# Block-sparse attention with a mixture of experts: the transposing product of the row maxima one step later, its rows masked by GpSimd

## The chip, the cores and the metric

The kernel runs on one core of a Trainium2 chip. The metric is the device time of one execution in microseconds (us); the time before is the median of three runs. The engines are called PE (TensorE, matrix products; PEld is its weight load), DVE (VectorE), ACT (ScalarE), POOL (GpSimd) and SP (SyncE, which issues most transfers). Each engine works through its own instructions in the order in which the program lists them, and waits on semaphores for the others.

## The reference

Attention over four batches, eight heads, 768 rows and 64 columns a head, then a mixture of eight experts of which each row takes two:

```python
scores = scale * np.matmul(q, k.transpose(0, 1, 3, 2))
mask = np.abs(blk_i - blk_j) <= 1          # blocks of 32, and first and last rows and columns of blocks
for qb in range(n_blocks):
    for kb in sampled_blocks[qb]:          # three sampled blocks a row of blocks
        mask[qb * block:(qb + 1) * block, kb * block:(kb + 1) * block] = True
scores = np.where(mask, scores, -1000000000.0)
scores = scores - np.max(scores, axis=-1, keepdims=True)
attn = np.exp(scores)
attn = attn / (np.sum(attn, axis=-1, keepdims=True) + 1e-09)
x = np.matmul(attn, v)                     # then rows of 512, over the heads
...
noisy_logits = x @ w_gate + noise * np.log1p(np.exp(x @ w_noise))
out[rows of e] += weight * (np.maximum(x @ w1[e], 0.0) @ w2[e])   # the two best experts of each row
```

## The kernel before

The class Attention computes the scores transposed, keys on partitions and query rows along the free dimension, so that exp(scores) can go straight into the product with v as the stationary operand. The maximum of each query row must therefore be known before, and it enters through the score product itself: q2 and k2 have extra contraction rows. Rows 64 to 87 carry the block mask, row 88 a constant, and rows MR = 96 to 101 carry the maxima: row 96 + t of q2 holds the maxima of the query tile t (128 rows) in the columns of that tile and zero in the others, against a constant -64 in k2.

There are 192 steps, six for each of 32 heads; two heads are a group, and 12 steps a group's turn. What a step n does stands in the loop of `steps` (lines 417 to 472), and this listing is the order in which every engine gets its instructions:

- `exp(n, 0)` and `exp(n, 1)` (lines 268 to 280): the scores of one tile of 128 keys against three tiles of query rows each, two products (L277, L279; the second reads k2 and q2 with the maxima) into a PSUM buffer pe (three of them), and ACT's exponential of it (L280).
- `max_mm(m)` (lines 228 to 238): two products (L234, L235) for the maxima of a later query tile m, into a PSUM buffer pm (two of them), and a relu of one half by ACT (L237). `max_red(m)` (lines 240 to 247): DVE adds the halves and takes the maximum along the row (L244) into one column of mn, a tile of 128x128 float16 per head (three of them).
- `halve(n)` (line 285): DVE turns the exponentials into float16.
- `av(n - 3)` (line 311): the product with v, 18 times three parts. Where n - 3 is the last step of a head (n % 6 = 2), this product comes first in the step and not behind `exp(n, 1)`; it then follows that of the step before without a score product between them.
- `av_end`: the end of a head: PSUM copied by ACT, sum and reciprocal (L326, L328) and scaling (L331) by DVE, a high part by ACT and a low part by GpSimd (L340).
- For later groups: casts (ACT, L206, and GpSimd, L208, one step later), transposes and copies by transfers from SP, the split of v (ACT, and DVE at L185) and differences of k (DVE, L254).

The maxima run ahead of the scores by LM = T + 3 = 9 steps (lines 68, 414 and 429; T = 6 query tiles a head): step n makes those of tile n + 9. When the sixth tile of a head has been reduced, `max_red` puts the head on the list `full` (line 247), with mn and the pm buffer of that last tile. In the next step (n % 6 = 3, three steps ahead of the head's first scores), behind the next tile's `max_mm`, `row_mm` (lines 256 to 260) transposes mn by a product with the identity into the free columns 384 to 511 of that same pm buffer (L260), and at the end of the step, behind `max_red` and `halve`, `row_put` (lines 262 to 266) has DVE read the six rows from PSUM, six times over, multiply them with a diagonal of the identity, and write the 6x768 values into q2 (L265). `start` (lines 396 to 402) does the same in the prologue, for the first eight tiles.

Between these parts `background(n, spot)` is called at four spots of a step. At spots 0 to 2 it advances a generator, Router.run, which computes the routing of one batch and ends with twelve indirect transfers by GpSimd (L695, each behind a small memset, L694) that scatter slots into a table in memory. The generator is advanced once a spot, and twice from step 158 to step 173 (lines 1060 to 1063); between two scatters it yields five times, for the third batch twice. At spot 3 the plan of `at(...)` is carried out: at step 169 a memset by GpSimd (L735), at step 178 the load of the first experts' table rows (L786), from step 180 on the indices made of them (DVE, L799) and the gathers of rows (GpSimd, L815).

Behind the attention the experts run one after the other (class Experts); this part holds over half of the span and is not changed.

Of the kernel before, what the change touches and what calls it, by code (L numbers as in the profile page):

```python
# [9 lines left out]
F32 = mybir.dt.float32  # L10
F16 = mybir.dt.float16
# [5 lines left out]
ALU = mybir.AluOpType  # L17
AX = mybir.AxisListType
PSUM = bass.MemoryType.PSUM
P = 128  # L20
# [24 lines left out]
class Attention:  # L45
# [16 lines left out]
    def __init__(self, tc, q, k, v, sampled):  # L62
        self.tc, self.nc = tc, tc.nc
        self.q, self.k, self.v, self.sampled = q, k, v, sampled
        self.B, self.H, self.S, self.D = q.shape
        self.T = self.S // P
        self.NB = self.S // 32
        self.LM = self.T + 3
        self.NG = self.B * self.H // self.G
        self.NSTEP = self.B * self.H * self.T  # L70
        self.st = {}
        self.todo = {}
        self.full = []
        self.now = 0

    def open(self, ctx, early):
# [151 lines left out]
    def max_mm(self, n):  # L228
        g, h, t = self.where(n)
        r = self.st[g]  # L230
        K = 64 + self.NB
        pm = self.ps_m.tile([P, 2, 512], F32, name="pm")
        q = r["q2"]
        self.nc.tensor.matmul(pm[:, 0, 0:384], q[0:K, h, t, :], r["k2"][0:K, h, 0::2, :], start=True, stop=True)  # L234
        self.nc.tensor.matmul(pm[:, 1, 0:384], q[0:K, h, t, :], r["kd"][0:K, h], start=True, stop=True)  # L235
        rl = self.sm.tile([P, 384], F32, name="rl")
        self.nc.scalar.activation(rl, pm[:, 1, 0:384], AF.Relu)  # L237
        self.st["pm", n] = pm, rl

    def max_red(self, n):  # L240
        g, h, t = self.where(n)
        pm, rl = self.st.pop(("pm", n))
        mn = self.mn[(n // self.T) % 3]
        self.nc.vector.tensor_tensor_reduce(rl, pm[:, 0, 0:384], rl, 1.0 / 64.0, -3.0e38, ALU.add, ALU.max,  # L244
                                            accum_out=mn[:, self.MR + t:self.MR + t + 1])
        if t == self.T - 1:
            self.full.append((g, h, mn, pm))

    def diff(self, g, hs):
        D = self.D  # L250
# [2 lines left out]
        k = r["k1" if g else "k2"][0:D, hs].rearrange("p g (j w) c -> p g j w c", w=2)  # L253
        self.nc.vector.tensor_tensor(kd[0:D, hs], k[:, :, :, 1], k[:, :, :, 0], op=ALU.subtract)  # L254

    def row_mm(self):
        self.rows, self.full = self.full, []
        n = self.MR + self.T
        for g, h, mn, pm in self.rows:
            self.nc.tensor.matmul(pm[0:n, 0, 384:512], mn[:, 0:n], self.ident, start=True, stop=True)  # L260

    def row_put(self):
        T, s = self.T, slice(self.MR, self.MR + self.T)
        for g, h, mn, pm in self.rows:
            self.nc.vector.tensor_tensor(self.st[g]["q2"][s, h], pm[s, 0, None, 384:512].to_broadcast([T, T, P]),  # L265
                                         self.ident[s, s, None].to_broadcast([T, T, P]), op=ALU.mult)

    def exp(self, n, x):
        nc, T = self.nc, self.T
        g, h, c = self.where(n)  # L270
        r = self.st[g]
        if x == 0:
            self.st["p32", n] = self.pi.tile([P, T, P], I32, name="p32")
        p32 = self.st["p32", n]
        t = slice(3 * x, 3 * x + 3)
        pe = self.psum()
        nc.tensor.matmul(pe[:, 0:384], r["k1"][:, h, c, :], r["q1"][:, h, t, :], start=True, stop=False)  # L277
        K = self.MR + T
        nc.tensor.matmul(pe[:, 0:384], r["k2"][0:K, h, c, :], r["q2"][0:K, h, t, :], start=False, stop=True)  # L279
        nc.scalar.activation(p32[:, t].rearrange("p t c -> p (t c)"), pe[:, 0:384], AF.Exp, scale=0.125)  # L280
# [12 lines left out]
    def later(self, steps, f):  # L293
        if steps:
            self.todo.setdefault(self.now + steps, []).append(f)
        else:
            f()
# [46 lines left out]
    def start(self, mi):  # L344
        nc, D, NB = self.nc, self.D, self.NB
        s32 = self.sampled.bitcast(I32)
        sb = mi.tile([P, NB * 3, 2], I32, name="sb")
        nc.scalar.dma_start(sb.rearrange("p a b -> p (a b)"),
                            bass.AP(tensor=s32.tensor, offset=s32.offset, ap=[[0, P], [1, NB * 6]]))
        nc.scalar.preload_act_table_set("natural_log_exp_and_others")  # L350
        r = self.st[0] = {nm: self.raw.tile([P, self.G, self.T, D], F32, name="raw_" + nm) for nm in "kq"}
        for h in range(self.G):
            for nm, src in (("q", self.q), ("k", self.k)):
                nc.sync.dma_start(r[nm][:, h], src[0, h].rearrange("(p t) d -> p t d", p=P))
        self.load(1, nc.sync, "kq")
        self.masks(mi, sb)
        self.constants(True)
        kn, qn = self.nat[0]
        kb, qb = self.kb, self.qb
        r["k2"], r["q2"] = self.k2[0], self.q2[0]  # L360
        self.new(r, "k1")
        self.new(r, "q1")
        cast = lambda dst, src: nc.scalar.activation(dst, src, AF.Copy)

        def high(h):
            cast(qb[:, h, :, 0:D], r["q"][:, h])
            cast(kb[:, h, :, 0:D], r["k"][:, h])

        def both(h):
            nc.gpsimd.tensor_sub(kn[:, h, :, D:], r["k"][:, h], kb[:, h, :, 0:D])  # L370
            nc.gpsimd.tensor_sub(qn[:, h, :, 0:D], r["q"][:, h], qb[:, h, :, 0:D])
            cast(kn[:, h, :, 0:D], r["k"][:, h])
            cast(qn[:, h, :, D:], r["q"][:, h])

        high(0)
        self.turn(r["q2"], qb, 0, "AA")
        both(0)
        high(1)
        both(1)
        self.load(0, None, "v")  # L380
        self.split(1, 0)
        self.split(1, 1)
        self.constants(False)
        self.split(1, 2)
        self.split(1, 3)
        self.turn(r["k2"], kb, 0, "AD")
        self.diff(0, slice(0, 1))
        more = {0: [(self.turn, r["k1"], kn, 0, "AD"), (self.load, 1, None, "v")],
                1: [(self.turn, r["q1"], qn, 0, "AD"), (self.load, 2)],
                2: [(self.turn, r["q2"], qb, 1, "AD")],  # L390
                3: [(self.turn, r["k2"], kb, 1, "AD")],
                4: [(self.diff, 0, slice(1, 2)), (self.load, 3)],
                5: [(self.vsplit, 0, 0)],
                6: [(self.turn, r["k1"], kn, 1, "AD"), (self.vsplit, 0, 1)],
                7: [(self.turn, r["q1"], qn, 1, "AD")]}
        for n in range(self.T + self.XM):
            self.max_mm(n)
            self.row_mm()
            self.max_red(n)
            self.row_put()  # L400
            for f, *a in more.get(n, ()):
                f(*a)
        self.flush()
        for t, m in ((self.k2, self.MR + self.T), (self.q2, self.MR)):
            nc.sync.dma_start(t[1][D:m], t[0][D:m])
        self.split(1, 4)
        self.split(1, 5)
        self.nmax = self.T + self.XM
        self.plan = {0: [(self.vsplit, 0, 2)], 2: [(self.diff, 1, slice(0, self.G))], 3: [(self.load, 2, None, "v")],
                     4: [(self.vsplit, 1, 0)], 5: [(self.vsplit, 1, 1)], 6: [(self.vsplit, 1, 2)],  # L410
                     9: [(self.vsplit, 2, 0)], 10: [(self.vsplit, 2, 1), (self.load, 3, None, "v")], 11: [(self.vsplit, 2, 2)],
                     1: [(nc.sync.dma_start, t[2][D:m], t[0][D:m]) for t, m in ((self.k2, self.MR + self.T), (self.q2, self.MR))]}
# [4 lines left out]
    def steps(self, on_group, background):  # L417
        NSTEP, LM, LA, GT = self.NSTEP, self.LM, self.LA, self.G * self.T
        for n in range(NSTEP + LA + 6 + self.ROWLATE):
            g, i = divmod(n, GT)  # L420
# [15 lines left out]
                self.exp(n, 0)  # L436
            self.av_end(j, "copy", on_group)
            self.av_end(j - 3, "high", on_group)
            for m in new:
                self.max_mm(m)  # L440
            self.row_mm()
# [3 lines left out]
                self.av(j)  # L445
            background(n, 0)
            self.av_end(j - 1, "sum", on_group)
            for m in new:
                self.max_red(m)
            if n < NSTEP:  # L450
                self.halve(n)
            self.row_put()
            background(n, 1)
            self.av_end(j - 1, "inverse", on_group)
            background(n, 2)
# [734 lines left out]
```

## Time and profile before

| | |
|---|---|
| median of 3 runs | 985.88 us |
| lowest and highest | 981.26 and 986.39 us |
| the profiled execution | 973.13 us, span 971.3 us |
| mean granted TensorE clock | 0.973 |
| PE busy | 876.8 us (90%) |
| DVE busy | 524.2 us (54%) |
| ACT busy | 454.6 us (47%) |
| POOL busy | 346.2 us (36%) |
| row matmul, L260 on PE | 32 times, 259 ns each, 32.6 us of idle time ahead of it |
| masked write into q2, L265 on DVE | 32 times, 962 ns each |
| halving, L285 on DVE | 192 times, 642 ns each |

The shares are means over the whole span, in which the attention and the experts have different limits; the text below goes by stretches. In a row of the waits stands who waited, for which line, and then the sum in us, the times and the longest one. In a row of the groups and of the timeline the operation is followed by output <- inputs, by shape, and in brackets by the idle time ahead of it and what ended that. In a row of a stretch stand the busy us of PE, PEld, DVE, ACT and POOL (with the number of instructions), then the granted clock, the share of the DMA engines and GB/s. Durations of matmuls are modelled: they overlap, and the distance between two starts is the time that each takes.

### The profile page before, as it was taken

What the parts mean: (1) busy time and instruction counts of PE and PEld (TensorE: products, weight loads), DVE (VectorE), ACT (ScalarE), POOL (GpSimd) and SP (SyncE); (2) the same over time, 40 slices, a digit from 0 to 9 for tenths busy, and PEclk for the clock granted to TensorE, in tenths of its full rate; (3) what the DMA queues carried; (4) which work ended last, traced back from release to release, by engine and by line L of the source; (5) the groups of instructions that cost most, each with busy time, mean ns of one, the idle gap of its engine ahead of it and who ended that gap; (6) DMA issues with size and microseconds to landing.
All of it is one profiled execution on the core that took longest, in us unless ns stands there. A gap on an engine that the chain in (4) does not pass through costs nothing. (4 is left out here: it accounts for less than half of the span.)

```text
span 971.3 us, 21082 instructions
## 1 busy us (share of the span) xinstructions
PE 876.8 (90%) x8493; PEld 530.2 (55%) x8493; DVE 524.2 (54%) x1238; ACT 454.6 (47%) x973; POOL 346.2 (36%) x392
## 2 busy tenths in 40 slices
PE   4888998989889887997799999999999999999993
PEld 2566665666566665645455555554554554555541
DVE  6888889989999974744023334333334333333210
ACT  6988888898889784522023123122221231231200
POOL 5432232552264163254242242342432432432220
PEclk9999999999999998997899999999999999999997
DMA  7678776796699288675859378297394593782210
GB/s 204 134 173 190 180 170 154 152 176 165 153 165 175 62 116 149 216 109 140 154 126 240 97 201 180 79 235 171 92 253 120 128 230 108 162 215 97 57 39 31
DMA packets 206618, 145.63 MB, mean 150 GB/s; under 512 B 142197, under 2 KB 183413, under 8 KB 206512
## 3 DMA queue, kind: packets, MB, share of 16 engines
q1 hardware_dynamic: 172848, 78.49, 40.0%
q0 software_dynamic: 14256, 39.58, 13.9%
q10 hardware_dynamic: 19408, 26.13, 11.1%
q8 instruction: 68, 1.11, 0.5%
q14 instruction: 38, 0.31, 0.1%
HBM read 79.62 MB, written 26.32 MB: 109 GB/s over the span
## 5 line engine op out<-in xcount | busy, mean ns | idle before, releaser
L280 ACT ACTIVATE p<-pe 128x384 int32<-128x384 f32 x384 | 189.7, 516 | 43.6 <-PE pe L279 36.9
L869 ACT ACTIVATE hh<-ph 128x408 f16<-128x408 f32 (+2 forms) x136 | 66.8, 492 | 273.7 <-PE ph L864 227.0
L870 DVE SCALAR_TENSOR_TENSOR hl<-ph,hh 128x408 f16<-128x408 f32 (+2 forms) x136 | 76.2, 561 | 180.1 <-ACT hh L869 180.1
L914 POOL DMA_INDIRECT out_dram<-y,mt x56 | 72.9, 1301 | 227.0 <-DVE y L912 105.1
L311 PEld LDWEIGHTS <-p 128*128 128x128 f16 x3456 | 128.5, 99 | 23.1 <-issue 1.7
L884 PEld LDWEIGHTS <-hh 128*128 128x128 f16 x768 | 75.0, 98 | 99.7 <-issue 14.4
L277 PE MATMUL pe<-q,k 128*128 128x384 f16 x384 | 128.2, 334 | 1.4 <-DVE r_A L649 1.0
L279 PE MATMUL pe<-q,k 102*128 102x384 f16 x384 | 128.2, 334 | 0.0
L285 DVE TENSOR_SCALAR p<-p 128x1536 f16<-128x1536 uint16 x192 | 123.3, 642 | 7.3 <-ACT p L280 5.8
L912 DVE SCALAR_TENSOR_TENSOR y<-py,mt,pv 128x512 f32<-128x512 f32 (+2 forms) x56 | 41.2, 748 | 157.9 <-PE py L884 142.2
L244 DVE CUSTOM_DVE_ANT_0 rl<-pm,rl 128x384 f32<-128x384 f32 x192 | 105.9, 552 | 34.3 <-ACT rl L237 30.7
L311 PE MATMUL po<-vx,p 128*128 128x65 f16 x1152 | 123.3, 196 | 0.4 <-DVE p L285 0.4
L311 PE MATMUL po<-vb,p 128*128 128x65 f16 x1152 | 123.0, 195 | 0.0
L311 PE MATMUL po<-vl,p 128*128 128x64 f16 x1152 | 122.8, 194 | 0.0
L864 PE MATMUL ph<-xta,w1hb 128*128 128x408 f16 x512 | 111.0, 340 | 7.3 <-issue 4.3
L237 ACT ACTIVATE rl<-pm 128x384 f32<-128x384 f32 x192 | 99.4, 518 | 11.2 <-PE pm L235 9.5
L830 POOL DMA_INDIRECT pv<-out_dram,gi x56 | 56.7, 1012 | 99.5 <-ACT hh L869 78.6
L864 PE MATMUL ph<-xtb,w1ha 128*128 128x408 f16 (+1 forms) x448 | 91.3, 325 | 0.3 <-DMA xtb<-xg 0.3
L884 PE MATMUL py<-w2ha,hh 128*128 128x512 f16 x192 | 73.9, 385 | 8.5 <-DVE y L912 8.5
L234 PE MATMUL pm<-k,q 88*128 88x384 f16 x192 | 64.7, 337 | 14.3 <-DVE mn L244 10.3
L340 POOL TENSOR_TENSOR x<-xr,x 128x384 f16<-128x384 f32 x32 | 34.5, 1078 | 119.0 <-ACT x L338 108.5
L864 PEld LDWEIGHTS <-w1hb 128*128 128x128 f16 x512 | 50.5, 99 | 47.0 <-issue 6.2
(192 smaller groups left out, 1616.5 us busy)
## 6 DMA issues: line engine op xcount, KB each, us to landing
wraw<-in_moe_w_dram SPq DMA_DIRECT2D x60, 512.0 KB, 4.2
raw_v<-in_v_dram ACTq DMA_DIRECT2D x16, 384.0 KB, 4.2
out_dram<-zero ACTq DMA_DIRECT2D x24, 256.0 KB, 3.6
x_rows<-x SPq DMA_DIRECT2D x16, 384.0 KB, 5.8
raw_k<-in_k_dram ACTq DMA_DIRECT2D x14, 384.0 KB, 3.8
raw_q<-in_q_dram ACTq DMA_DIRECT2D x14, 384.0 KB, 6.8
k<-k SPq DMA_DIRECT2D x15, 192.0 KB, 3.7
q<-q SPq DMA_DIRECT2D x15, 192.0 KB, 3.8
```

What stands on the lines that cost most here:

```text
L237: self.nc.scalar.activation(rl, pm[:, 1, 0:384], AF.Relu)
L244: self.nc.vector.tensor_tensor_reduce(rl, pm[:, 0, 0:384], rl, 1.0 / 64.0, -3.0e38, ALU.add, ALU.max, accum_out=mn[:, self.MR + t:self.MR ...
L277: nc.tensor.matmul(pe[:, 0:384], r["k1"][:, h, c, :], r["q1"][:, h, t, :], start=True, stop=False)
L279: nc.tensor.matmul(pe[:, 0:384], r["k2"][0:K, h, c, :], r["q2"][0:K, h, t, :], start=False, stop=True)
L280: nc.scalar.activation(p32[:, t].rearrange("p t c -> p (t c)"), pe[:, 0:384], AF.Exp, scale=0.125)
L285: self.nc.vector.tensor_scalar(p.rearrange("p t c w -> p (t c w)"), p32.bitcast(U16).rearrange("p t c -> p (t c)"), HC, None, op0=ALU.mult)
L311: self.nc.tensor.matmul(o, p[:, t, :, w], v, start=first and i == 0, stop=last and i == 2, skip_group_check=True)
L864: nc.tensor.matmul(ph[:, b, 0:m], w[wt][:, kb, fs], r["xt"][:, kb, a, o:o + m], start=i == 0, stop=i == last)
L869: self.pace = nc.scalar.activation(hv, ph[:, b, 0:m], AF.Relu)
L870: nc.vector.scalar_tensor_tensor(self.hl[:, f, o:o + m], ph[:, b, 0:m], 0.0, hv, op0=ALU.max, op1=ALU.subtract)
L884: nc.tensor.matmul(py, h[:, f, o], w[x][:, f, :], start=i == 0, stop=i == last)
L914: nc.gpsimd.indirect_dma_start(out=self.out, out_offset=bass.IndirectOffsetOnAxis(ap=r["mt"][0:m, c, 0:1], axis=0), in_=y[0:m], in_offset= ...
```

## The change

The transposing product is made one step later than before, as the first thing in a pm buffer that the step's own maxima need anyway; a head's entry now ages by one step on the list before it is due. So that it is still done three steps ahead of the head's scores, the maxima run one step further ahead (LM = T + 4). In the loop, DVE copies the six rows out of PSUM into a small float16 tile, ahead of the step's maximum (`row_copy`, behind the first background spot), and GpSimd multiplies them with the diagonal and writes q2. The prologue keeps DVE's `row_put`, one pass later.

```diff
-        self.LM = self.T + 3
+        self.LM = self.T + 4
...
-        self.full = []
+        self.full, self.due, self.rows = [], [], []
...
         pm = self.ps_m.tile([P, 2, 512], F32, name="pm")
+        self.row_mm(pm)
         q = r["q2"]
...
         if t == self.T - 1:
-            self.full.append((g, h, mn, pm))
+            self.full.append((1, g, h, mn))
...
-    def row_mm(self):
-        self.rows, self.full = self.full, []
+    def age(self):
+        self.due += [e[1:] for e in self.full if not e[0]]
+        self.full = [(0, *e[1:]) for e in self.full if e[0]]
+
+    def row_mm(self, pm=None):
         n = self.MR + self.T
-        for g, h, mn, pm in self.rows:
+        for g, h, mn in self.due:
+            pm = pm or self.ps_m.tile([P, 2, 512], F32, name="pm")
             self.nc.tensor.matmul(pm[0:n, 0, 384:512], mn[:, 0:n], self.ident, start=True, stop=True)
+            self.rows.append((g, h, pm))
+        self.due = []
 
     def row_put(self):
         T, s = self.T, slice(self.MR, self.MR + self.T)
-        for g, h, mn, pm in self.rows:
+        for g, h, pm in self.rows:
             self.nc.vector.tensor_tensor(self.st[g]["q2"][s, h], pm[s, 0, None, 384:512].to_broadcast([T, T, P]),
                                          self.ident[s, s, None].to_broadcast([T, T, P]), op=ALU.mult)
+        self.rows = []
+
+    def row_copy(self):
+        T, s = self.T, slice(self.MR, self.MR + self.T)
+        for g, h, pm in self.rows:
+            tm = self.sm.tile([P, P], F16, name="tm", bufs=2)
+            self.nc.vector.tensor_copy(tm[s], pm[s, 0, 384:512])
+            self.nc.gpsimd.tensor_tensor(self.st[g]["q2"][s, h], tm[s, None, :].to_broadcast([T, T, P]),
+                                         self.ident[s, s, None].to_broadcast([T, T, P]), op=ALU.mult)
+        self.rows = []
...
         for n in range(self.T + self.XM):
+            self.age()
             self.max_mm(n)
-            self.row_mm()
             self.max_red(n)
...
             self.av_end(j - 3, "high", on_group)
+            self.age()
             for m in new:
                 self.max_mm(m)
             self.row_mm()
...
             self.av_end(j - 1, "sum", on_group)
+            self.row_copy()
             for m in new:
                 self.max_red(m)
             if n < NSTEP:
                 self.halve(n)
-            self.row_put()
             background(n, 1)
```

## The prediction

> **What bounds the kernel now.** I read the page first, then the stretches of the span, then the waits inside the attention loop.
>
> ```profile
> span 971.3 us, 21082 instructions
> PE   4888998989889887997799999999999999999993
> DVE  6888889989999974744023334333334333333210
> 200.00:250.00 50.00, 45.09 (x695) 32.17 (x693) 45.52 (x136) 43.31 (x106) 18.19 (x21) 0.97 0.78 162
> ```
>
> One slice is 24.3 us. The attention is the part where VectorE (DVE) reads 8 or 9 and a little beyond (the last halving, quoted below, starts at 382.1); the change touches nothing behind it. In the stretch from 200 to 250 us PE is busy 45.1 of 50 us, DVE 45.5, ScalarE (ACT) 43.3 and GpSimd (POOL) 18.2. Three engines are nearly full, so the waits decide. From 40 to 345 us:
>
> ```profile
> PEld L260 <- DVE mn L244: 35.1, 25, 2.2
> DVE rl L244 <- ACT rl L237: 25.8, 26, 1.4
> PE pm L260 <- DVE mn L244: 25.4, 25, 1.8
> PE pm L234 <- DVE mn L244: 9.1, 15, 1.2
> ```
>
> PE waits for DVE alone: at the row matmul (L260), once per head, and at the maxima (L234), for one of their two PSUM buffers. DVE waits once per head too, about 1.0 us each, for the relu. One head in order of time, PE, then DVE, then ACT:
>
> ```profile
> 206.14 0.32 PE L235 MATMUL pm<-kd,q 88*128 88x384 f16 x1
> 207.11 0.26 PE L260 MATMUL pm<-ident,mn 128*102 128x128 f16 x1 [0.64 <-DVE mn L244]
> 211.47 0.33 PE L234 MATMUL pm<-k,q 88*128 88x384 f16 x1
> ...
> 207.63 0.56 DVE L244 CUSTOM_DVE_ANT_0 rl<-pm,rl 128x384 f32<-128x384 f32 x1
> 208.25 0.56 DVE L285 TENSOR_SCALAR p<-p 128x1536 f16<-128x1536 uint16 x1
> 208.84 0.96 DVE L265 TENSOR_TENSOR q<-pm,ident 6x768 f16<-6x768 f32 x1
> 209.84 0.19 DVE L328 RECIPROCAL rc<-rc 128x6 f32<-128x6 f32 x1
> 210.72 0.56 DVE L244 CUSTOM_DVE_ANT_0 rl<-pm,rl 128x384 f32<-128x384 f32 x1
> ...
> 208.99 0.48 ACT L237 ACTIVATE rl<-pm 128x384 f32<-128x384 f32 x1
> ```
>
> PE could go on about 0.16 us after 206.14 (the duration shown is twice the step from one such matmul to the next), so the head loses 207.11 - 206.30 = 0.8 us. The relu that starts at 208.99 is ready at 209.47, but the maximum that reads it starts at 210.72: behind the row step DVE is the late engine, by 1.2 us.
>
> **The wait that goes.** The transposing matmul will read maxima that are two steps old, ahead of maxima for which PE must have the buffer anyway. I take its wait away whole: 0.8 us per head here, 25.4 + 25 x 0.16 = 29 us over the stretch. It is a gain only if nothing else is late.
>
> **What DVE does instead.** It loses the masked write of 1.00 us (208.84 to 209.84) and gets a copy of 128 elements out of PSUM; GpSimd gets the mask, 6x768, two inputs. Neither is in the trace. The nearest rows:
>
> ```profile
> L569 DVE COPY r_lc<-pe 128x192 f32<-128x192 f32 x3 | 1.1, 355 | 0.1
> L122 DVE CAST k<-pe 128x384 f16<-128x384 f32 x4 | 2.2, 556 | 1.0 <-PE pe L117 1.0
> 10.58 1.64 POOL L208 TENSOR_TENSOR kn<-raw_k,kn 128x768 f16<-128x768 f32 x1
> 12.18 1.75 POOL L208 TENSOR_TENSOR qn<-raw_q,qn 128x768 f16<-128x768 f32 x1
> 202.67 1.38 DVE L285 TENSOR_SCALAR p<-p 128x1536 f16<-128x1536 uint16 x1
> 202.69 0.92 POOL L340 TENSOR_TENSOR x<-xr,x 128x384 f16<-128x384 f32 x1
> ```
>
> The copy: (556 - 355) / 192 = 1.05 ns an element, so 355 - 64 x 1.05 = 0.29 us. The mask: two inputs and 768 elements took GpSimd 1.64 and 1.75 us; with half as many elements it took 0.92. The mask has float16 inputs on six partitions, which could be faster, so its bounds are 0.9 and 1.75 us. I take 1.65, the row with its element count.
>
> The last two rows say more. The halving of p (L285) starts beside a GpSimd operation and ends at 204.05, 0.44 us after GpSimd did at 203.61: DVE is held for the whole of it. Free of that it takes:
>
> ```profile
> L285 DVE TENSOR_SCALAR p<-p x192: 544/556/1740, 26.6 to 382.1; 128x1536 f16<-128x1536 uint16 x192
> L244 DVE CUSTOM_DVE_ANT_0 rl<-pm,rl x192: 537/557/561, 14.1 to 367.6; 128x384 f32<-128x384 f32 x192
> ```
>
> The halving's longest is 1.74 us, the maximum's (one input in PSUM) 0.56: GpSimd holds the one and not the other. The mask starts right after the copy, and the halving follows the maximum about 0.5 us later, so each mask meets one.
>
> Put into the head above: copy 207.63 to 207.92, maximum from 207.95, mask 208.0 to 209.65 (0.1 us is my allowance for the signal), halving held until then and done at 210.1. Now DVE reaches that point at 209.84, so it is 0.25 us later, not 0.7 earlier. The next maximum moves to 210.97 and ends at 211.55. PE, 0.8 us early without the wait, is at the matmul of 211.47 by 210.67, finds both buffers full and waits to about 211.6. Of the 0.8 us nothing is left: +0.1 us per head. With a mask of 0.9 us the halving is done at 209.35, the next maximum ends at 210.8, and some 0.7 us stays. So a head lies between -0.7 and +0.3 (held twice, by the mask and by the casts' GpSimd work that the mask pushes later); I take +0.1, by the 768-element row: 28 x 0.1 = +3 us.
>
> Two rules of the Trainium skill would price the mask differently. "Perfetto Trace Analysis", section "GPSIMD Instruction", calls a GpSimd span unreliable and times by the distance of starts: 12.18 - 10.58 = 1.60 us, which takes 0.05 us off a head. "GPSIMD Engine Reference", section 4.1 "Engine selection", advises against GpSimd for elementwise work, about 2x slower for two inputs: from the 0.96 us of L265 that makes an estimated 1.9 us and adds 0.25 us per head, 7 us in all; the rows above give 1.7 to 1.8 times.
>
> **GpSimd's queue.** The mask is also moved onto an engine that works in program order. Mostly that is harmless: GpSimd is busy 18 of 50 us and q2 is read three steps later. Not near the end of the loop, where the third batch's twelve slot scatters (L695) come three to a step:
>
> ```profile
> 337.56 1.61 POOL L695 DMA_INDIRECT slots<-r_pay,r_sl  x1 [13.01 <-DVE r_ot L687]
> 355.00 0.97 POOL L695 DMA_INDIRECT slots<-r_pay,r_sl  x1 [0.22 <-issue]
> 344.55 0.96 DVE L265 TENSOR_TENSOR q<-pm,ident 6x768 f16<-6x768 f32 x1
> 347.01 0.33 PE L279 MATMUL pe<-q,k 102*128 102x384 f16 x1
> 366.56 0.17 DVE L799 TENSOR_SCALAR gi<-mt 128x5 int32<-128x5 int32 x1 [5.62 <-DMA mt<-slots]
> ```
>
> By the generator's yields (two calls a spot from step 158 on, two yields a scatter) the twelfth scatter is issued in the first spot of step 171. The mask of step 171, the one of 344.55 now, comes right behind it in the queue. GpSimd is busy with that chain until 355.97, so this mask ends at 357.6 instead of 345.5. The score matmul of step 174 that reads it is at 347.01: a stall of 10.6 us, in which all three engines run empty. Part comes back: at step 180 DVE now waits 5.62 us, to 366.56, for the table that these scatters fill; shifted by 10.6 us it gets there at 371.5, when the table is in. Net +5 us. The last mask (step 183) stands behind five gathers of the experts' rows, from the first of these rows to the last:
>
> ```profile
> 367.01 1.04 POOL L815 DMA_INDIRECT xg<-x_rows,gi  x1 [7.43 <-DVE gi L799]
> 372.79 1.00 POOL L815 DMA_INDIRECT xg<-x_rows,gi  x1 [0.30 <-issue]
> ```
>
> That is 6.8 us, with the mask 8.4, and its reader is three steps away: 0 to 3 us, of which I count 0, since the experts' start waits for the same gathers.
>
> Then the prologue:
>
> ```profile
> 21.49 0.96 DVE L265 TENSOR_TENSOR q<-pm,ident 6x768 f16<-6x768 f32 x1
> 23.95 0.55 DVE L244 CUSTOM_DVE_ANT_0 rl<-pm,rl 128x384 f32<-128x384 f32 x1
> 23.23 0.52 PE L279 MATMUL pe<-q,k 102*128 102x384 f16 x1
> ```
>
> There the masked write stays on DVE but moves from the seventh pass to the eighth, behind the maximum of 23.95. That one gains its 1.0 us (22.95 to 23.5), the write ends at 24.5, and the first score matmul of 23.23 waits for it: +1.3 us at most, since PE soon waits for DMAs; I take 1.
>
> The lead of one more step (LM) means an extra pair of maxima at step 3, which moves work and adds none, and maxima that need k2, q2 and kd one step sooner; these are issued five steps ahead, and I count 0. The age lists cost nothing on the chip.
>
> **Sum.** 3 + 5 + 1 = +9 us. The profiled execution took 973.13 us (971.3 span), 12.75 below the median 985.88 of the three runs; as a shift that makes 982 for a profile and about 995 for the median.
>
> **The rivals.**
> *The mask is short (faster).* If it takes about 0.9 us, or ends while DVE waits for the relu anyway, a head gains 0.4 to 0.7 us and 28 heads 11 to 20; with the 6 us of queue and prologue the time is 972 to 981, about 976. For it: float16 inputs, and the 25.8 us in which DVE idles. Against: that idle lies ahead of the maximum one step before the copy, and the rows with float16 beside float32 show no such speed. It decides from a mask under about 1.2 us.
> *No stall in the queue (no change).* If the mask of step 171 gets ahead of the scatters, or the chain ends sooner, only 0 to 4 us remain: about 988.
> *Held twice (slower still).* If the pushed casts hold DVE a second time in each head, +0.3 us each: 28 x 0.3 + 6 = 14 us, about 1001 with the last mask's wait.
>
> **How the numbers follow.** Forecast 0.44, short mask 0.24, no stall 0.18, held twice 0.14. Under 0.5% a measurement of this kernel cannot tell a change, so the bounds are 981 and 991. Faster takes the short mask, 0.24. Same takes the missing stall and the forecast's lower tail, 0.18 + 0.09 = 0.27. Slower takes the rest, 0.49. Faster and slower both hold much, so: the forecast's own range is 988 to 1000, and the range for 8 in 10 is 975 to 1002.
>
> **What would show it.** Right: no wait of L260's successor for the maxima; waits of PE at L234 for DVE growing from 9 to 20 us or more; a GpSimd mask of 1.6 to 1.75 us x30; a mean of L285 well above its median of now, 556 ns; one wait of the score matmul for GpSimd's q2 of about 10 us near 350 us; the wait of L799 gone. Wrong: masks near 0.9 us, L285 unchanged, waits at L234 as now, or the step of 174 without a stall. The attention then ends earlier than now, and the time is under 981.

## The result, and the profile after

Slower, and by more than the range allowed: 1022.81 us median (1020.93 to 1030.21, 6 runs) against 982.26 us (980.30 to 986.39, 6 runs) of the kernel before, a ratio of 1.042 [1.038, 1.046], or 40.5 us; the brackets behind a ratio are its 95% interval. The forecast was 995 us, 975 to 1002. The profiled execution of the changed kernel took 1022.69 us, 49.6 us more in the span than the one before. That one took 973.13 us, 9 us less than the median of its kernel's runs, so the traces show 9 us more than the medians. The page of the changed kernel:

```profile
span 1020.9 us, 21189 instructions
PE   4888888788777867788689999999999999999992
DVE  6888889878986865373312333333333333333310
```

One slice is now 25.5 us. Among PE's first 20 digits there are eight 7s and 6s, the first of them at the eighth digit (179 us); before there were three. The waits between 40 and 345 us (what waited, for whom, us in total, times, longest):

```profile
PE pm L235 <- DVE mn L245: 25.5, 28, 3.0
...
PE pe L296 <- POOL q L281: 14.3, 7, 4.1
...
PE pm L265 <- DVE mn L245: 2.0, 3, 0.7
...
POOL q L281 <- DMA slots<-r_pay,r_sl: 26.1, 7, 5.7
```

The wait of the row matmul (L260 before, L265 now) fell from 25.4 to 2.0 us, and that of the maxima (L234, now L235) rose from 9.1 to 25.5, as predicted. The other two rows are new: the score matmul waits for GpSimd's q2, and GpSimd's mask waits for the slot scatters. Now the new instructions by the tile tm, and the halving (min/median/max in ns):

```profile
L280 DVE CAST tm<-pm x31: 296/297/298, 34.1 to 407.8; 6x128 f16<-6x128 f32 x31
L281 POOL TENSOR_TENSOR q<-tm,ident x31: 1465/1467/1732, 34.5 to 415.3; 6x768 f16<-6x768 f16 x31
```

```profile
L302 DVE TENSOR_SCALAR p<-p 128x1536 f16<-128x1536 uint16 x192 | 149.0, 776 | 14.8 <-ACT p L297 12.2
```

Copy 0.30 us, mask 1.47 us; the halving's mean is 776 ns where it was 642 (123.3 us over 192, now 149.0). In order of time, first one undisturbed head on DVE and GpSimd, then the places where the time goes:

```profile
80.86 0.30 DVE L280 CAST tm<-pm 6x128 f16<-6x128 f32 x1
81.31 1.47 POOL L281 TENSOR_TENSOR q<-tm,ident 6x768 f16<-6x768 f16 x1 [6.16 <-DVE tm L280]
81.67 1.52 DVE L302 TENSOR_SCALAR p<-p 128x1536 f16<-128x1536 uint16 x1
...
193.95 1.72 POOL L713 DMA_INDIRECT slots<-r_pay,r_sl  x1 [0.18 <-issue]
201.41 1.56 POOL L281 TENSOR_TENSOR q<-tm,ident 6x768 f16<-6x768 f16 x1 [5.74 <-DMA slots<-r_pay,r_sl]
203.02 0.48 PE L296 MATMUL pe<-q,k 102*128 102x384 f16 x1 [3.61 <-POOL q L281]
...
382.54 0.96 POOL L713 DMA_INDIRECT slots<-r_pay,r_sl  x1 [0.23 <-issue]
388.02 1.47 POOL L281 TENSOR_TENSOR q<-tm,ident 6x768 f16<-6x768 f16 x1 [4.52 <-issue]
389.54 0.48 PE L296 MATMUL pe<-q,k 102*128 102x384 f16 x1 [14.56 <-POOL q L281]
...
403.94 0.17 DVE L817 TENSOR_SCALAR gi<-mt 128x5 int32<-128x5 int32 x1
415.26 1.47 POOL L281 TENSOR_TENSOR q<-tm,ident 6x768 f16<-6x768 f16 x1 [4.43 <-DMA xg<-x_rows,gi]
416.78 0.48 PE L296 MATMUL pe<-q,k 102*128 102x384 f16 x1 [4.19 <-POOL q L281]
```

At 81.67 the halving starts 0.36 us into the mask, and it ends at 83.19, 0.41 us after the mask: held, as predicted. Before 201.41 GpSimd has idled for 5.74 us, since the issue of a scatter ended; it is not its own queue that it waits for, but the landing of the transfer. The same stands before the mask of 388.02 (4.52 us after the twelfth scatter's issue; the profile names no releaser there) and, with the gathers, of 415.26. In the compiled program a mask lists, among what it waits for, the semaphore of every indirect transfer that GpSimd issued since the mask before; 12 of the 31 masks have such an entry. The casts and low parts on GpSimd (L208, L357), on all 128 partitions, list none, and in the trace before the change they follow a scatter at once:

```profile
180.51 1.09 POOL L695 DMA_INDIRECT slots<-r_pay,r_sl  x1 [0.18 <-issue]
181.63 0.92 POOL L340 TENSOR_TENSOR x<-xr,x 128x384 f16<-128x384 f32 x1
```

The start of each head's mask (before: of DVE's masked write) gives the loss by stage. Where the two kernels do it in a step differs by a constant, which the first row holds. The columns to the right belong to experiments below, on chips where the kernel before had medians of 971 to 972 us; a stage of 140 us may differ by 1.5 us for that alone. From head 1 to head 13 it did not: the run with scatters in steps 3 and 4 (below), which up to there has the instructions of the changed kernel, took the same 138.22 us on one of those chips.

| stage (heads) | before | changed | changed less before | stand-ins | one tile |
|---|---|---|---|---|---|
| span's start to 1 | 32.42 | 34.52 | +2.1 | 35.03 | 35.35 |
| 1 to 13 | 133.02 | 138.22 | +5.2 | 135.53 | 128.12 |
| 13 to 26, the scatters of two batches | 144.19 | 163.14 | +19.0 | 151.68 | 153.03 |
| 26 to 28 | 23.84 | 24.45 | +0.6 | 24.45 | 22.84 |
| 28 to 29, the third batch's twelve scatters | 11.08 | 27.69 | +16.6 | 18.25 | 24.90 |
| 29 to 31 | 25.79 | 27.24 | +1.4 | 27.77 | 25.65 |
| 31 to the end | 600.96 | 605.64 | +4.7 | not compared | 602.61 |

### The profile page after: what moved, and what is told of

The parts are those of the page before. It is cut to its first block, busy times and chain, and to the rows that moved or that the text cites. A ratio compares the mean times of both kernels' runs of the same rounds, so it can differ in the third digit from the quotient of the medians.

```text
span 1020.9 us, 21189 instructions
## 1 busy us (share of the span) xinstructions
PE 889.1 (87%) x8493; PEld 539.3 (53%) x8493; DVE 531.4 (52%) x1238; ACT 452.5 (44%) x973; POOL 400.6 (39%) x423
## 5 line engine op out<-in xcount | busy, mean ns | idle before, releaser
L297 ACT ACTIVATE p<-pe 128x384 int32<-128x384 f32 x384 | 192.9, 526 | 73.9 <-PE pe L296 64.5
L296 PE MATMUL pe<-q,k 102*128 102x384 f16 x384 | 129.8, 338 | 35.8 <-POOL q L281 33.8
L302 DVE TENSOR_SCALAR p<-p 128x1536 f16<-128x1536 uint16 x192 | 149.0, 776 | 14.8 <-ACT p L297 12.2
L328 PEld LDWEIGHTS <-p 128*128 128x128 f16 x3456 | 132.0, 100 | 26.5 <-issue 3.8
L328 PE MATMUL po<-vx,p 128*128 128x65 f16 x1152 | 126.5, 198 | 1.9 <-DVE p L302 1.7
L328 PE MATMUL po<-vb,p 128*128 128x65 f16 x1152 | 126.0, 197 | 0.0
L328 PE MATMUL po<-vl,p 128*128 128x64 f16 x1152 | 125.9, 196 | 0.0
L238 ACT ACTIVATE rl<-pm 128x384 f32<-128x384 f32 x192 | 99.1, 517 | 12.6 <-PE pm L236 10.1
L281 POOL TENSOR_TENSOR q<-tm,ident 6x768 f16<-6x768 f16 x31 | 46.0, 1483 | 133.4 <-DVE tm L280 89.0
L235 PE MATMUL pm<-k,q 88*128 88x384 f16 x192 | 65.6, 342 | 33.6 <-DVE mn L245 30.5
L882 PEld LDWEIGHTS <-w1ha 128*128 128x128 f16 x576 | 57.1, 100 | 42.4 <-issue 4.0
```

Of the source, the lines that this page charges most:

```text
L302: self.nc.vector.tensor_scalar(p.rearrange("p t c w -> p (t c w)"), p32.bitcast(U16).rearrange("p t c -> p (t c)"), HC, None, op0=ALU.mult)
L328: self.nc.tensor.matmul(o, p[:, t, :, w], v, start=first and i == 0, stop=last and i == 2, skip_group_check=True)
L882: nc.tensor.matmul(ph[:, b, 0:m], w[wt][:, kb, fs], r["xt"][:, kb, a, o:o + m], start=i == 0, stop=i == last)
```

## The experiments

**Landing theory**: the mask waits until GpSimd's indirect transfers have landed, and the score matmuls wait for the mask; this makes most of the loss. **Queue-and-hold theory**, the prediction's: GpSimd's queue is only in order, and DVE's halving is held. A third, **order theory**: the later product and the extra step of maxima cost the time. Each "changed kernel" below is the kernel after the change.

**Stand-ins for the scatters.**

```diff
...
                 nc.gpsimd.memset(self.spacer, 0.0)
+                if b <= self.B - 2:
+                    nc.gpsimd.memset(self.standin, 0.0)   # 128x1024 f16
+                    for _ in range(self.SF if b == self.B - 2 else self.SN):
+                        yield
+                    continue
```

> Edit: the changed kernel, with each scatter of the first three batches replaced by a GpSimd memset of 128x1024 f16 (0.98 us by the row of such a memset; a scatter takes 1.01 us): these batches' table entries are left out, so that the work after attention is not the reference's, and only the heads up to 400 us are compared. The queue keeps its length and its order, and the mask has no scatter to wait for. Landing theory: head 13 to 17 takes 44 to 47 us (43.4 before, 53.8 in the changed kernel), head 21 to 26 takes 56 to 59 us (54.8, 63.7), head 28 to 29 about 23 us (11.1, 27.7). Queue theory (GpSimd's order alone): each within 1.5 us of the changed kernel's.

One profiled execution, 989.48 us. On GpSimd and PE, in order of time:

```profile
205.44 1.47 POOL L281 TENSOR_TENSOR q<-tm,ident 6x768 f16<-6x768 f16 x1 [0.96 <-DVE tm L280]
...
364.94 1.66 POOL L281 TENSOR_TENSOR q<-tm,ident 6x768 f16<-6x768 f16 x1
366.65 0.48 PE L296 MATMUL pe<-q,k 102*128 102x384 f16 x1 [3.87 <-POOL q L281]
```

The mask now waits for DVE's copy alone, and in the burst for nothing: it stands right behind twelve memsets. Head 13 to 17 took 46.2 us and head 21 to 26 took 56.4 (216.71 - 170.56 and 322.24 - 265.88), as the landing theory has it. Head 28 to 29 took 18.25, less than its 23: the stand-ins also do without the scatters' own wait for their indices, which was 3.46 us ahead of the first scatter of that burst in the changed kernel. By head 31 the changed kernel is 44.9 us later than the kernel before (415.26 - 370.34), this one 22.4. So about half of the loss up to head 31 is waiting for transfers (up to some 5 us of it the shorter burst), and 7.2 of the rest is the burst's plain queue (18.25 - 11.08).

**The mask of one tile.**

```diff
...
-            self.nc.gpsimd.tensor_tensor(self.st[g]["q2"][s, h], tm[s, None, :].to_broadcast([T, T, P]),
-                                         self.ident[s, s, None].to_broadcast([T, T, P]), op=ALU.mult)
+            self.nc.gpsimd.tensor_tensor(self.st[g]["q2"][s, h, 0:1], tm[s, None, :].to_broadcast([T, 1, P]),
+                                         self.ident[s, s.start:s.start + 1, None].to_broadcast([T, 1, P]), op=ALU.mult)
```

> Edit: the changed kernel with the mask of one of the six tiles only (6x128 in place of 6x768); the maxima of the other five tiles are left out of q2 (zeros there). The mask then takes some 0.3 to 0.5 us in place of 1.47 us, DVE's halving is hardly held, and the waits for landings are as they were. Landing theory: only the hold's 0.43 us a head goes, 12 us of 28 heads: 1007 to 1015 us, with waits of 10 to 15 us of the score matmul for q2 still there. Queue-and-hold theory (the mask's own length): 982 to 992 us.

992.08 us, ratio 1.020 [1.014, 1.026]; on that chip the kernel before took 971.8 us, so the expectations, as ratios to 982.26 us, are 1.025 to 1.033 for the landing theory and 1.000 to 1.010 for the other. It fell between. Groups (count, then us in all and mean ns, then idle time ahead and its releasers):

```profile
L304 DVE TENSOR_SCALAR p<-p 128x1536 f16<-128x1536 uint16 x192 | 124.4, 648 | 12.9 <-ACT p L299 12.2
L283 POOL TENSOR_TENSOR q<-tm,ident 6x128 f16<-6x128 f16 x31 | 12.9, 418 | 137.8 <-DVE tm L282 93.7 <-DMA slots<-r_pay,r_sl 14.6 <-DVE mn L247 8.6
L298 PE MATMUL pe<-q,k 102*128 102x384 f16 x384 | 129.4, 337 | 34.2 <-POOL q L283 32.2 <-DVE q L274 2.1
```

The score matmul's wait for q2 is as long as in the changed kernel, where the row of the same group has 33.8 us. The hold is gone (648 ns), and the stage without scatters, head 1 to 13, is 10.1 us shorter than in the changed kernel and 4.9 shorter than before: without the hold, DVE's 0.30 us in place of 0.96 is a gain of 0.6 us a head. So both causes are there: with a short mask the waits for landings stay, and about half of the net loss goes with the hold, which in the changed kernel takes the copy's gain back.

**The halves of the change.** The product back in the step of its last maxima, copy and mask kept:

```diff
-        self.LM = self.T + 4
+        self.LM = self.T + 3
...
-            self.age()
             for m in new:
                 self.max_mm(m)
             self.row_mm()
```

> Edit: the changed kernel with the product in the step of its head's last maxima, behind them, and with the maxima one step less ahead, as before the change; the copy by VectorE and the mask by GpSimd stay. It parts the change's two halves. Landing theory: the mask has the same waits at about the same time, and PE has its wait for the last maximum (0.8 us a head) again, which lay beside DVE's work: 1018 to 1030 us. Order theory (the later product and the extra step of maxima ahead cost the time): 982 to 992 us.

1009.66 us, ratio 1.038 [1.031, 1.045]: the loss stays, and the order theory falls. PE has its wait for the last maximum again (24.9 us in 27 waits of the row matmul), and the masks their waits for scatters:

```profile
L276 POOL TENSOR_TENSOR q<-tm,ident 6x768 f16<-6x768 f16 x31 | 45.4, 1465 | 127.0 <-DVE tm L275 83.4 <-DMA slots<-r_pay,r_sl 16.8 <-DVE p L297 8.1
```

The other half, the later product with DVE's write at its old place at the end of the step:

```diff
-            self.row_copy()
             for m in new:
                 self.max_red(m)
             if n < NSTEP:
                 self.halve(n)
+            self.row_put()
```

> Edit: the changed kernel's product, one step later and ahead of the maxima, but VectorE writes q2 straight from PSUM at the old place at the end of the step; no copy, no mask, nothing of it on GpSimd. DVE theory (DVE is the late engine in every head, so PE's wait for the last maximum cost nothing): the same as before the change, ratio 0.995 to 1.004. Rival (PE's 0.8 us a head is on the path): ratio 0.975 to 0.985. Order theory (the later product itself costs): ratio above 1.02.

964.13 us against 971.20, ratio 0.993 [0.990, 0.996]: faster than both kernels, between the two expectations. Heads 4 to 10 take 10.44 us each, before the change 10.67: of PE's 0.8 us a head, 0.2 is worth something. By PE's waits, what keeps the rest is its buffer for the maxima, which DVE's write now gives back:

```profile
L235 PE MATMUL pm<-k,q 88*128 88x384 f16 x192 | 64.6, 337 | 36.1 <-DVE q L272 19.8 <-DVE mn L245 12.4 <-ACT k L120 3.0
```

**Scatters in steps 3 and 4 alone, meant to keep them away from the masks.**

```diff
+                while b < self.B - 2 and self.att.now % 6 not in (3, 4):
+                    yield
...
-                for _ in range(self.SF if b == self.B - 2 else self.SN):
+                for _ in range(self.SF if b <= self.B - 2 else self.SN):
```

> Edit: the changed kernel, but the first two batches issue their scatters only in steps 3 and 4 of a head's six, two steps or more ahead of the next mask, so that they have landed by then; the third batch's burst and the gathers are as they were. Landing theory: the +10.4 us and +8.9 us of the first two batches go, so 1001 to 1009 us. Queue-and-hold theory: as many instructions in the same queue, 1018 to 1026 us.

1010.97 us, ratio 1.041 [1.035, 1.047]: no gain beyond the noise. But the waits had not gone:

```profile
L281 POOL TENSOR_TENSOR q<-tm,ident 6x768 f16<-6x768 f16 x31 | 47.1, 1519 | 131.3 <-DVE tm L280 93.4 <-DMA slots<-r_pay,r_sl 17.4 <-DVE mn L245 7.9
```

The named waits for scatters are 17.4 us where the changed kernel has 26.1, but all the idle time ahead of the ten masks that list scatters of the first two batches is 30.0 us where it was 33.0. The edit does not do what the expectation says. A scatter that was held back goes out at the first spot of step 3, and that spot stands ahead of the mask of the same step: in the trace the last scatter starts 2.3 to 5.8 us before such a mask, not two steps or more. The run missed its aim and does not tell the theories apart.

**The mask at partition 0, carried to its rows by a transfer.**

```diff
...
+            tq = self.sm.tile([P, T, P], F16, name="tq", bufs=2)
+            self.nc.vector.tensor_copy(tm[0:T], pm[0:T, 0, 384:512])
+            self.nc.gpsimd.tensor_tensor(tq[0:T], tm[0:T, None, :].to_broadcast([T, T, P]),
+                                         self.ident[0:T, 0:T, None].to_broadcast([T, T, P]), op=ALU.mult)
+            self.nc.sync.dma_start(self.st[g]["q2"][s, h], tq[0:T])
```

> Edit: the changed kernel, but the product puts its six rows at partitions 0 to 5, the copy and GpSimd's mask work there on a tile of their own, and SyncE carries the 6x768 result to q2's rows 96 to 101 by a DMA. In the program this mask has no wait for GpSimd's own scatters and gathers, where the mask at partitions 96 to 101 has one for each of them since the mask before; its size, its engine and its place in GpSimd's queue are unchanged, and q2 is still read by the score matmuls. Landing theory (the mask waits until GpSimd's indirect DMAs have landed, and the score matmuls wait for the mask): the two early batches' +19 us and most of the third batch's +17 us go, the held halving's 0.43 us a head stays: 983 to 997 us. Queue-and-hold theory (the prediction's: GpSimd is in order, and DVE's halving is held during the mask): nothing goes, 1015 to 1030 us.

1021.57 us, ratio 1.052 [1.045, 1.059]: not the landing theory's number, and a little above the other's. The reason is a third:

```profile
L299 PE MATMUL pe<-q,k 102*128 102x384 f16 x384 | 132.5, 345 | 59.9 <-DMA q<-tq 58.6 <-DVE q L273 1.3
...
L283 POOL TENSOR_TENSOR tq<-tm,ident 6x768 f16<-6x768 f16 x31 | 45.5, 1469 | 115.0 <-DVE tm L282 114.9
```

GpSimd's wait for landings is gone (all but 0.1 us of its idle time is for DVE's copy). The added transfer takes its place: the score matmuls wait 58.6 us for that. The time is inconclusive; the next pair asks the question without a reader.

**Beside DVE's own write, a copy and a mask that nobody reads**, on partitions 0 to 5 and on 96 to 101. Against the run with the late write:

```diff
...
+            tm = self.tmf[h]
+            self.nc.vector.tensor_copy(tm[0:T], pm[0:T, 0, 384:512])      # or tm[s], pm[s]: 96 to 101
+            self.nc.gpsimd.tensor_tensor(self.idle[0:T], tm[0:T, None, :].to_broadcast([T, T, P]),
+                                         self.ident[0:T, 0:T, None].to_broadcast([T, T, P]), op=ALU.mult)
```

> Edit: the run with VectorE's late write of q2 (ratio 0.993), and beside it the changed kernel's copy and GpSimd mask, on partitions 0 to 5, into a tile that nobody reads. PE waits for neither. It prices the pair's load on VectorE: 0.30 us for the copy and 0.96 us (1.52 less 0.56) for the halving that is held during the mask. Hold theory: DVE is the late engine, so 1.0 to 1.25 us a head for 30 heads, 30 to 38 us: ratio 1.02 to 1.035, mean halving 0.78 us. Rival (the hold lies beside other waits): ratio 0.995 to 1.005. GpSimd has no wait for landings.

> Edit: the same with the unread copy and mask on partitions 96 to 101; nothing else differs. Landing theory: GpSimd idles 25 to 45 us in front of these masks for scatters and gathers to land, as in the changed kernel, and in the run on partitions 0 to 5 not at all; as nobody reads the mask, the time is the same within 1% or up to 2% longer, by what else in GpSimd's queue comes late. Rival (the waits come from the result's readers or from q2, not from where the mask starts): no such idle time in either.

1021.78 us, ratio 1.052 [1.047, 1.057], and 1024.11 us, 1.052 [1.046, 1.058]. The mask's group on partitions 0 to 5, then on 96 to 101:

```profile
L283 POOL TENSOR_TENSOR idle<-tmf,ident 6x768 f16<-6x768 f16 x31 | 45.5, 1466 | 110.7 <-DVE tmf L282 110.6
```

```profile
L283 POOL TENSOR_TENSOR idle<-tmf,ident 6x768 f16<-6x768 f16 x31 | 46.2, 1492 | 130.2 <-DVE tmf L282 80.6 <-DMA slots<-r_pay,r_sl 21.4 <-DVE p L303 15.4
```

That settles where the landing wait comes from: not from q2 and not from a reader, but from the partition on which the operation starts. In the first program no mask lists a scatter, in the second those behind scatters do. And while nobody reads the result, the wait costs nothing that the two ratios show. What the pair costs was far over the expectation, 58.7 us of span against the late write (1017.6 - 958.9). PE on partitions 0 to 5, two heads in order of time:

```profile
86.95 0.34 PE L237 MATMUL pm<-k,q 88*128 88x384 f16 x1 [1.78 <-DVE q L274]
...
98.66 0.34 PE L237 MATMUL pm<-k,q 88*128 88x384 f16 x1 [2.12 <-DVE q L274]
98.83 0.39 PE L238 MATMUL pm<-kd,q 88*128 88x384 f16 x1
99.01 0.53 PE L295 MATMUL pe<-q,k 128*128 128x384 f16 x1
...
102.24 0.40 PE L297 MATMUL pe<-q,k 102*128 102x384 f16 x1
...
103.02 0.33 PE L295 MATMUL pe<-q,k 128*128 128x384 f16 x1
```

DVE's 0.30 us and a hold of about 1 us stand here on top of the 0.96, and the wait comes at the maxima. A head without more takes 11.7 us, 1.26 over the late write's. After the wait of 2.12 us PE's matmuls follow each other at 0.32 us in place of 0.16 for 3.4 us (98.83 to 102.24), and such heads take 12.8 to 13.0 us. The mean granted clock is 0.956 against 0.978. Of 23 waits of PE of 1.5 to 2.7 us between 40 and 400 us, 12 were followed by such a stretch within 8 us; of nine waits of 0.8 to 1.3 us none. The Trainium skill, "TensorE: Matmul & The Clock Gate", section "What's actually happening", has a window of 3.4 us, running freely, after which an idle PE gets half its clock: the length and the rate agree with this trace, and that equal waits differ fits a free-running window. The same page of the Trainium skill, section "Why this matters for your kernels", asks for no gaps over about 3 us; here 1.6 to 2.6 us did it half the time.

**Without GpSimd.** The rows of one tile copy carried by one transfer into a single row of q2, where no mask is needed; on SyncE's and on ScalarE's queue, then one and two steps earlier on SyncE's:

```diff
-            self.nc.gpsimd.tensor_tensor(self.st[g]["q2"][s, h], ...)
+            self.later(1, lambda q=self.st[g]["q2"], h=h, tm=tm: self.nc.sync.dma_start(   # or scalar
+                q[self.MR:self.MR + 1, h], tm[s]))
...
-        K = self.MR + T
+        K = self.MR + (T if n < T else 1)
...
-        self.LM = self.T + 4
+        self.LM = self.T + 5    # or 6; the third and the fourth run alone
```

> Edit: the changed kernel with GpSimd's mask left out: VectorE's copy of the product's six rows (0.30 us) stays, and a step later SyncE's queue moves them by one DMA of six 256-byte rows into one row of q2 (row 96, 1x768), so that no mask is needed; the score matmul of these heads reads 97 rows in place of 102. DVE's work falls by 0.66 us a head against the kernel before (0.96 to 0.30), and no halving is held. DVE theory: about 0.6 us a head for 30 heads goes: ratio to before 0.975 to 0.987. Rival (the DMA's way takes the mask's place): score matmuls wait for q2 from the DMA, ratio 1.00 to 1.02.

> Edit: as the run before, with the DMA issued on ScalarE's queue, where an issue of a load takes 0.37 to 0.45 us. DVE theory: the same 0.6 us a head less, ratio 0.975 to 0.99. Rival (ScalarE is as late as VectorE, so 0.4 us a head comes back, and it waits at the issue): ratio 0.99 to 1.01.

> Edit: the run with the row moved by a DMA on SyncE's queue, with the maxima and so the product one more step ahead (LM = T + 5), which gives the DMA one step (1.7 us) more. There the score matmul waited 18 times for the DMA, 35.8 us in all, most of them 1 to 2.7 us. Lead theory (the DMA's 4.5 us from issue to landing is what is late): most of these waits go, some 20 us: ratio to before 0.985 to 0.993. Rival (a DMA that is late will be late by as much wherever it is put, behind the groups' transposes on its queue): ratio above 1.003.

> Edit: as the run before with two more steps ahead (LM = T + 6). Lead theory: all waits but the two long ones (7.2 and 4.3 us) go, 0.6 us a head of DVE's work is left as the gain: ratio 0.978 to 0.988. Rival (the maxima now come before the next group's operands are there, so the wait moves to the maxima matmuls): ratio 1.00 or above.

Ratios 1.010 [1.007, 1.013], 1.014 [1.011, 1.017], 1.023 [1.016, 1.031] and 1.012 [1.007, 1.018]: no gain in any. In the first, SyncE issues as soon as the copy (86.00 to 86.30) is done, and the score matmul still waits:

```profile
86.32 0.76 SPq L281 DMA_DIRECT2D q<-tm  x1
...
91.04 0.48 PE L296 MATMUL pe<-q,k 97*128 97x384 f16 x1 [2.39 <-DMA q<-tm]
```

Issue to use is 4.7 us for 1.5 KB. The early heads without that wait took 9.9 to 10.1 us, which is DVE's 0.6 us. On ScalarE's queue the waits for the transfer fall from 35.8 to 15.5 us, and PE waits for ScalarE's exponentials instead, which is the rival's mechanism (its range ended at 1.01):

```profile
L294 PE MATMUL pe<-q,k 128*128 128x384 f16 x384 | 127.3, 332 | 12.8 <-ACT p L297 9.9 <-ACT q L120 0.4
```

With one step more than in the first run the transfer's waits did not fall (38.8 us, 35.8 there), against the lead theory. The transfers themselves came later: between 60 and 330 us, where PE waited for one, its use lay 2.6 to 5.7 us behind its issue in the first run and 3.5 to 8.8 us here. With two steps the waits went, and another appeared at the differences of k:

```profile
L296 PE MATMUL pe<-q,k 97*128 97x384 f16 (+1 forms) x384 | 128.5, 335 | 3.0 <-DVE q L272 2.1 <-DMA q<-tm 1.0
L236 PE MATMUL pm<-kd,q 88*128 88x384 f16 x192 | 65.0, 339 | 23.1 <-DVE kd L255 23.1
```

Why the transfers came later with one step more, and two brought it all, stays open.

## Why the prediction was wrong

That the change is slower was right. The size was not, because the sum held no term for the wait that cost most.

**The wait that goes, and the copy: right.** 0.29 us for the copy was 0.30; the row matmul's wait went.

**DVE held by the mask: right, sizes close.** The mask was taken at 1.65 us and took 1.47. From head 3 to head 10 the changed kernel needs 10.88 us a head against 10.67 ((135.62 - 59.47) / 7 and (130.12 - 55.45) / 7): +0.21 in place of +0.1, inside the bounds, 6 us in 28 heads in place of 3. The late write adds what the prediction could not see: that the wait of 0.8 us had 0.2 us of worth which the copy and the hold took back.

**GpSimd's queue: the step that failed.** The prediction took the mask to wait for its turn in the queue and for nothing else. It put it as "Mostly that is harmless: GpSimd is busy 18 of 50 us and q2 is read three steps later. Not near the end", and gave the queue net +5 us. An instruction behind a scatter was taken to be free once the scatter was issued, as the low parts (L340) in the trace are. The mask, on partitions from 96, is free once the scatter has landed; in the seven named waits that was 3.6 to 7.5 us after the last scatter's issue began. So the two batches counted at zero cost +19.0 us in their stage; with the third batch's 16.6 that is 35.6 of the 49.6 us. The stand-ins take 11.5 of the 19.0 away. Of the 7.5 that stay, 13 heads at 0.21 explain 2.7, and 2.3 fall into one head, 20 to 21 (14.37 us against 12.05 before), in which PE had a granted clock of 0.50 to 0.53 from 258 to 264 us. The rest stays open.

**The third batch's burst.** A stall of 10.6 us was forecast from the queue alone, and 14.56 us was measured, the last 4.52 of them for the landing; the 10.0 us of the queue were right. DVE's wait of 5.62 us for the table did go (L817 at 403.94 has none), but the time was not given back: head 29 to 31 took 1.4 us longer than before, not 5.6 shorter. The stage ends at the start of the last mask, and that mask's own wait of 4.43 us for the gathers lies in it; without it, some 3 of the 5.6 us had come back. With the plain queue, in the stand-ins, the burst is +7.2.

**The last mask.** 0 was counted, with a bound of 3; its wait for the gathers' landing made PE wait 4.19 us.

**Rivals.** "Held twice" had the number nearest to the result, by a mechanism that did not make the loss: the undisturbed heads lost 0.21 us each, 6 us in all. None of the rivals had the landing. The waits also cost clock. The mean granted clock fell from 0.973 to 0.957, and from 40 to 400 us from 0.98 to 0.94. In the changed kernel the score matmul's waits of 3.61, 4.13 and 14.56 us were each followed by a stretch in which PE was busy throughout at half its clock (a row of a stretch ends with the granted clock, the DMA share and GB/s):

```profile
203.00:207.00 4.00, 3.98 (x28) 2.43 (x28) 1.13 (x3) 2.37 (x5) 3.54 (x6) 0.50 0.03 5
315.30:319.40 4.10, 4.07 (x28) 2.43 (x28) 1.77 (x3) 1.98 (x5) 3.69 (x6) 0.50 1.02 259
389.50:393.00 3.50, 3.46 (x26) 2.15 (x26) 1.13 (x3) 1.51 (x4) 0.91 (x1) 0.50 0.39 70
```

Half of these stretches makes an estimate of some 6 us. The kernel before has such stretches too (granted clock 0.50 from 368.3 to 373.0 us), so how many of the 49.6 us are due to them stays open.

## What to carry to other kernels

An instruction that moves to another engine gets its own list of waits there; the neighbours' rows in the trace do not show it. On GpSimd, ask what indirect transfers it has issued, where the operation's partitions start, and who reads the result. Moving DVE work to GpSimd paid nothing here, since DVE's halving was held for as long as GpSimd ran; the only gain lay in the product's place (0.993), with the write left on DVE.

## What the runs showed that was not expected

- A GpSimd operation on partitions 96 to 101 waited for the landing of GpSimd's scatters (21.4 us in 5 named waits), the same on partitions 0 to 5 not at all. The wait stands in the program's list, so these runs say nothing on whether the chip needs it.
- PE waits of 1.6 to 2.6 us were, in 12 of 23 cases, followed by half-rate stretches, of 3.4 us in the one shown, and such heads took 12.8 to 13.0 us in place of 11.7.
- A transfer of 1.5 KB within the on-chip memory took 2.6 to 5.7 us from its issue to its use where PE waited for it, with the queues as busy as they are in this loop.
